# Window attention with a depthwise convolution: x loaded ahead of the convolution, LN by rows of seven tokens, its transposes in the convolution's PSUM banks

## The chip, the cores and the metric

The kernel runs on one core of one Trainium2 chip. A core has TensorE (PE, the matrix engine; PEld is its weight load), VectorE (DVE), ScalarE (ACT), GpSimd (POOL) and SyncE (SP), which here only issues DMAs. SBUF holds tiles of 128 partitions; PSUM holds the results of matmuls, in banks of 512 float32 per partition. The metric is the device time of one execution in microseconds (us), lower is better.

## The reference

The input is an image x of 511 x 511 pixels with 192 channels, in bfloat16. It gets a depthwise 3 x 3 convolution added, and then attention runs inside windows of 7 x 7 pixels, with four heads of 48 channels. The weights are `dw_pe` (3, 3, 192), `w_qkv` (192, 576) and `w_o` (192, 192).

```
xp = pad(x, 1 pixel on each side of H and W)
pe = sum over i, j in 0..2 of xp[:, i:i+H, j:j+W, :] * dw_pe[i, j]
x0 = x + pe
h  = (x0 - mean(x0)) / sqrt(var(x0) + 1e-5)        # over the 192 channels
h  = h cut into windows of 7 x 7                    # 73 x 73 = 5329 windows, 49 tokens each
q, k, v = split(h @ w_qkv)                          # 4 heads of 48
attn = softmax(einsum('wnhd,wmhd->whnm', q, k) * 48 ** -0.5)
out  = einsum('whnm,wmhd->wnhd', attn, v) @ w_o
return x0 + out, windows put back in place
```

## The kernel before

**Blocks.** The 5329 windows are cut into 42 blocks of up to 128 windows (the last has 81). A block's tile `X` is [128 windows, 49 tokens, 192 channels]; there are three of them, `X[b % 3]`. `XP` holds the 9 x 9 pixel patches of a block's windows, with the 81 pixels on the partitions, and `T` holds the convolution as 81 x 49 matrices, one for each channel. So the convolution of a block is 192 matmuls (L308), one a channel; ten of them fill a one-bank PSUM tile `psc` (a ring of two), and DVE casts that tile into `X` (L313).

**LN.** The LN of a block then runs in 7 rows of 7 tokens. For each, DVE adds x to the convolution (L320) from a small buffer `xs` (two of them, one DMA a row, L288), and takes statistics of two tokens at a time (L324, 25 a block). GpSimd turns the variances of sixteen tokens at once into reciprocal roots, with one multiply-add (L330) and one power of -0.5 (L331), and multiplies `X` by them (L339, eight tokens an instruction). The result goes to `X[(b + 1) % 3]`, whose content has been stored by then. The mean isn't subtracted: the weights are made so that it drops out. PE transposes the normalised tokens, eight at a time and in two halves of 96 channels (L353), into one PSUM tile `ps` of two banks (a ring of three, which all of attention uses), and both halves are copied into `HO[b % 2]` (L363), the first by DVE, the second by ACT. Six such steps of 16 transposes and one of two make the 98 of a block.

**Attention.** A block is worked in 16 slots of 8 windows. In a slot PE does, in this order: q (L375), the transposes of an output (E, L458) of two slots ago, k (L375), the output projection of the block before (L470, 13 a block, spread over slots 2 to 10), LN transposes for the next block, attention times v (D, L434) of the slot before, scores (B, L413), and the value projection (V, L391). Each of them takes the next `ps` of the ring. ACT copies q and k (L383) and v (L399) out of PSUM and takes the exponential (`pt`, L421). DVE takes the reciprocal of the sums (L443) and scales the outputs (`o`, L444). The transposed outputs are copied into `HO` (L459) by DVE in slots 0 to 7 and by ACT from slot 8 on (L616: `late = f0 >= 0.44`). A projection is copied by ACT to `pO` (L481; the last of a block has one token, L483), and added to `X` on GpSimd (L485).

**What sets the order.** The instructions are issued by hand in program order; each engine works its own in that order and waits on semaphores. While a block is attended to, the next one is prepared: `fill` puts its convolution matmuls between those of q, k and V, up to 0.44 of the slots; `hook(share)` is called at several places of a slot and issues the LN items (statistics, x loads, GpSimd's work), the stores of the block before (L293, four of them), and the 18 patch loads of the block after the next (L234), on SP's queue, as far as the slot's share says. A transposition is issued when its rows are at least 0.9 slots old.

Of the kernel before, what the change touches and what calls it, by code (L numbers as in the profile page):

```python
# [61 lines left out]
class _Kernel:  # L62
    def __init__(self, ctx, tc, x, dw_pe, w_qkv, w_o, out, eps, logit_lim):
# [24 lines left out]
        with tc.tile_pool(name="setup", bufs=1) as setup:  # L88
# [88 lines left out]
            for t in self.X:  # L177
                nc.gpsimd.memset(t[:], 0.0)
        for t in self.load_xp(0):
            t()  # L180
# [54 lines left out]


    def fast(self, ctx):
# [5 lines left out]
        bnst = pool.tile([128, 25, 6], F32, name="bnst")  # L243
        rstd = pool.tile([128, 50], F32, name="rstd")
        tmp1 = pool.tile([128, 50], F32, name="tmp1")
        expo = pool.tile([128, 50], F32, name="expo")
# [10 lines left out]
        for t in [k_] + xs.t:  # L257
            nc.vector.memset(t[:], 0.0)
# [18 lines left out]
        dram, load_xp = self.dram, self.load_xp  # L277

        def strips(b, r0, r1):

            for a0, b0, da, db, n, p0 in blocks[b]:
                yield slice(p0, p0 + n), (WS * a0 + r0, WS * b0, [[WS * C * (W * da + db), n], [W * C, r1 - r0], [1, WS * C]])

        CHUNKS = [(0, 2), (2, 4), (4, 6), (6, 7)]

        def load_x(b, r, t):
            for p, at in strips(b, r, r + 1):
                nc.sync.dma_start(out=t[p].rearrange("p (r q) c -> p r (q c)", q=WS), in_=dram(x, *at))  # L288
# [27 lines left out]


        def ln_add(b, r, t):
            xv = self.X[b % 3][:, r * WS : (r + 1) * WS, :]
            nc.vector.tensor_tensor(out=xv, in0=xv, in1=t[:], op=ALU.add)  # L320

        def ln_stat(b, i):
            s = min(2 * i, S - 2)
            nc.vector.bn_stats(out=bnst[:, i, :], in_=self.X[b % 3][:, s : s + 2, :].rearrange("p s c -> p c s"))  # L324

        def ln_rstd(i0, i1):
            v = bnst[:, i0:i1, :].rearrange("p a (e f) -> p a e f", f=3)[:, :, :, 2]
            rd, t = (z[:, 2 * i0 : 2 * i1] for z in (rstd, tmp1))
            e = nc.gpsimd
            e.tensor_scalar(out=t.rearrange("p (a e) -> p a e", e=2), in0=v, scalar1=1.0 / C, scalar2=self.eps, op0=ALU.mult, op1=ALU.add)  # L330
            e.tensor_tensor(out=rd, in0=t, in1=expo[:, 2 * i0 : 2 * i1], op=ALU.pow)  # L331

        def hbuf(b):
            return self.X[(b + 1) % 3]

        def ln_norm(b, s0, s1, eng=nc.gpsimd):
            assert b < 2 or stored.get(b - 2, 0) * 2 * WS >= s1 or stored.get(b - 2, 0) == len(CHUNKS)
            i, n = (49 if s0 == S - 1 else s0), s1 - s0
            eng.tensor_tensor(  # L339
                out=hbuf(b)[:, s0:s1, :],  # L340
                in0=self.X[b % 3][:, s0:s1, :],
                in1=rstd[:, i : i + n].unsqueeze(2).to_broadcast([128, n, C]),
                op=ALU.mult,
            )

        def ln_tr(b, s0, n):
            h = hbuf(b)
            ps = PS.next()
            pb = ps[:].bitcast(BF)
            N = min(8, S - s0)  # L350
            for kt in range(2):
                for i in range(N):
                    mm(  # L353
                        pb[0:KT, kt * 1024 + i * 128 : kt * 1024 + (i + 1) * 128],
                        lhsT=h[:, s0 + i, kt * KT : (kt + 1) * KT],
                        rhs=ident[:],
                        start=True,
                        stop=True,
                        is_transpose=True,
                    )  # L360
            for kt in range(2):
                eng = nc.vector.tensor_copy if kt == 0 else nc.scalar.copy
                eng(  # L363
                    out=HO[b % 2][0:KT, kt, :, s0 : s0 + N],
                    in_=pb[0:KT, kt * 1024 : kt * 1024 + N * 128].rearrange("p (s w) -> p w s", w=128),
                )
# [122 lines left out]

        def stat_items(b):  # L490

            tiles = {}
            items = []
            done = 0
            for r in range(WS):
                items.append((1, lambda r=r: ln_add(b, r, tiles[r])))
                last = 25 if r == WS - 1 else (r + 1) * WS // 2
                for i in range(done, last):
                    items.append((0, lambda i=i: ln_stat(b, i)))
                    if i % 8 == 7 or i == 24:  # L500
                        items.append((0, lambda i0=i // 8 * 8, i1=i + 1: ln_rstd(i0, i1)))
                        for s0 in range(i // 8 * 16, min(S, 2 * i + 2), 8):
                            items.append((2, lambda s0=s0: ln_norm(b, s0, min(S, s0 + 8), nc.vector if b == 0 and s0 % 16 else nc.gpsimd)))
                done = last
            return items, tiles

# [5 lines left out]
        class Next:  # L512


            def __init__(n_, b):
                n_.b, n_.conv, n_.si, n_.loaded, n_.tr = b, Conv(b), 0, 0, 0
                n_.items, n_.tiles = stat_items(b)
                n_.ready, n_.due, n_.added = [], [], 0

            def load(n_):  # L520
                if n_.loaded < WS:
                    n_.tiles[n_.loaded] = xs.next()
                    load_x(n_.b, n_.loaded, n_.tiles[n_.loaded])
                    n_.loaded += 1

            def stats(n_, goal):
                while n_.si < goal:
                    kind, it = n_.items[n_.si]
                    if kind == 1 and n_.loaded == n_.added:
                        n_.load()  # L530
                    it()
                    n_.si += 1
                    if kind == 1:
                        n_.added += 1
                    if kind == 2:
                        n_.ready.append(now[0])

            def transpose(n_, goal, age):

                if n_.tr < min(goal, len(n_.ready)) and n_.ready[n_.tr] + age <= now[0]:  # L540
                    ln_tr(n_.b, 8 * n_.tr, n_.tr)
                    n_.tr += 1
                    return True
                return False

        n = Next(0)
        n.load()
        n.load()
        while n.conv.c < C:
            conv_mm(n.conv)  # L550
        if NB > 1:
            for t in load_xp(1):
                t()
        n.stats(len(n.items))
        while n.tr < 7:
            n.transpose(7, -9.0)
        sq = []

        for g in range(NG + LE + 1):
# [6 lines left out]
            if ck == 0:  # L566
                n = Next(b + 1) if b + 1 < NB else None
                xp, xpn = (list(load_xp(b + 2)), 0) if b + 2 < NB else ([], 0)
                pdone = sdone = 0
# [11 lines left out]
            conv_goal = part(0.0, 0.44, C)  # L581
# [10 lines left out]
            s_goal = part(0.46, 0.82, len(n.items)) if n else 0  # L592

            def hook(share):

                nonlocal xpn, sdone
                at = f0 + (f - f0) * share
                if n and conv.c == C:
                    n.stats(int(s_start + (s_goal - s_start) * share))
                    if n.loaded < min(WS, n.added + 2):  # L600
                        n.load()
# [10 lines left out]
            if n and f0 >= 0.3 and n.loaded == 0:  # L612
                n.load()
                n.load()

            late = f0 >= 0.44  # L616
# [3 lines left out]
            if 0 <= g - LE < NG:  # L620
                stage_E(*groups[g - LE], nc.scalar.copy if late else nc.vector.tensor_copy)
# [10 lines left out]
            if n and g < NG:  # L632
                n.transpose(part(0.56, 0.96, 7), 0.9)
            if 0 <= g - LD < NG:
                stage_D()
            if g < NG:
# [3 lines left out]
                if n:  # L640
# [3 lines left out]
                    if f == 1.0:  # L644
                        while n.tr < 7:
                            n.transpose(7, -9.0)
                hook(1.0)
            if f == 1.0:
                while xpn < len(xp):
                    xp[xpn]()  # L650
                    xpn += 1
            if g >= NG:
                hook(1.0)
# [5 lines left out]
    def slow(self, ctx):  # L659
# [25 lines left out]
        nc.vector.memset(XP[:], 0.0)  # L685
# [215 lines left out]
```

## Time and profile before

| | |
|---|---|
| median of 3 runs (lowest to highest) | 4792.46 us (4783.4 to 4797.41) |
| the profiled execution's own time | 4794.51 us |
| its span (first to last instruction) | 4792.8 us |
| mean granted clock of PE, of full speed | 0.863 |
| PE busy | 3893.8 us, 81% |
| PEld busy (beside PE) | 3356.2 us, 70% |
| ACT busy | 3029.9 us, 63% |
| DVE busy | 2722.9 us, 57% |
| POOL busy | 2087.7 us, 44% |

The shares are means over stretches with different limits: a block begins with the convolution as filler for PE and goes on with the LN of the next block. The chain of work that ended last has PE on 56% of the span, ACT on 13%, DVE on 11% and POOL on 8%. Busy time of PE depends on its clock: the same matmuls take longer at the lower level, so a busy share can fall when the clock rises.

### The profile page before, as it was taken

The page shows a single profiled execution, that of the slowest core. Times are in us where ns is not written, and L with a number is a line of the kernel's source. Part 1 is how long each engine was busy: PE and PEld are TensorE (multiplying, and loading weights), DVE is VectorE, ACT ScalarE, POOL GpSimd, SP SyncE. Part 2 cuts the span into 40 slices and gives each one's busy share as a digit, 9 for nine tenths or more (in the row PEclk, how much of TensorE's full clock was granted, in tenths as well). Part 3 has the DMA queues.
Part 4 walks back from the last instruction along what each step waited for, and adds up shares of the span by engine and source line. Part 5 has one row for each costly group of instructions (what it writes and reads, how often), then busy time and mean ns, then how long its engine had stood idle before and what let it go on. Part 6 is the DMA issues. An engine that isn't in the chain of part 4 may idle for free.

```text
span 4792.8 us, 167033 instructions
## 1 busy us (share of the span) xinstructions
PE 3893.8 (81%) x75049; PEld 3356.2 (70%) x75049; DVE 2722.9 (57%) x4200; ACT 3029.9 (63%) x3842; POOL 2087.7 (44%) x1179
## 2 busy tenths in 40 slices
PE   2788888888888888888888888888888888878777
PEld 2677777777777777777777777777777777767665
DVE  5655555565555555555556555555555655555543
ACT  0566666666666666666666666666666666666555
POOL 5244444444444444444444444444444444444333
PEclk9899898888888899899888888889888888888888
DMA  3133333333333333333333333333333333333211
GB/s 93 50 76 76 76 87 81 90 86 89 86 83 76 76 76 76 76 87 82 86 82 87 92 87 76 76 76 76 76 83 80 89 85 77 87 86 78 67 45 35
DMA packets 529704, 376.98 MB, mean 79 GB/s; under 512 B 454181, under 2 KB 454373, under 8 KB 528979
## 3 DMA queue, kind: packets, MB, share of 16 engines
q1 hardware_dynamic: 528513, 365.92, 31.1%
q8 instruction: 589, 9.65, 0.8%
q14 instruction: 136, 1.11, 0.1%
q10 hardware_dynamic: 466, 0.30, 0.0%
HBM read 265.31 MB, written 100.27 MB: 76 GB/s over the span
## 4 chain that ended last, share of the span: by engine, by line
PE 56%; ACT 13%; DVE 11%; POOL 8%; issue 4%; SPq 4%; DMA 3%; ACTq 0%; DVEq 0%; POOLq 0%
PE ps L375 20%; PE ps L391 11%; PE psc L308 9%; PE ps L458 7%; ACT pO L481 6%; DVE HO L363 5%; POOL X L339 5%; ACT HO L363 5%; PE ps L353 4%; PE ps L470 4%; SPq L234 3%; DVE bnst L324 3%; DMA XP<-in_x_dram 3%; DVE X L320 2%; POOL X L485 2%
## 5 line engine op out<-in xcount | busy, mean ns | idle before, releaser
L485 POOL TENSOR_TENSOR X<-X,pO 128x768 bf16<-128x768 bf16 (+1 forms) x539 | 859.5, 1610 | 2322.9 <-ACT pO L481 2321.2
L375 PE MATMUL ps<-HO,Wqk 96*128 96x392 bf16 x5336 | 1632.4, 397 | 113.7 <-DVE o L444 76.2
L308 PEld LDWEIGHTS <-XP 81*128 81x128 bf16 x8064 | 1101.5, 177 | 164.9 <-issue 105.7
L391 PE MATMUL ps<-Wv,HO 96*128 96x192 bf16 x5336 | 718.0, 267 | 485.9 <-ACT HO L363 395.5
L308 PE MATMUL psc<-T,XP 81*128 81x49 bf16 x8064 | 1080.2, 221 | 37.4 <-DMA XP<-in_x_dram 28.2
L375 PEld LDWEIGHTS <-Wqk 96*128 96x128 bf16 x5336 | 656.0, 127 | 321.3 <-issue 211.2
L391 PEld LDWEIGHTS <-HO 96*128 96x128 bf16 x5336 | 556.4, 109 | 450.2 <-issue 419.0
L383 ACT CAST k<-ps 128x784 bf16<-128x784 f32 x667 | 542.8, 814 | 408.5 <-PE ps L375 370.2
L363 DVE COPY HO<-ps 96x1024 bf16<-96x1024 bf16 (+1 forms) x294 | 336.9, 1147 | 784.9 <-ACT k L383 402.5
L383 ACT CAST q<-ps 128x784 bf16<-128x784 f32 x667 | 542.0, 813 | 370.7 <-PE ps L375 329.1
L339 POOL TENSOR_TENSOR X<-X,rstd 128x1536 bf16<-128x1536 bf16 (+1 forms) x291 | 729.8, 2525 | 19.4 <-DMA out_dram<-X 6.2
L399 ACT CAST v<-ps 128x768 bf16<-128x768 f32 x667 | 535.2, 802 | 294.8 <-PE ps L391 262.4
L313 DVE CAST X<-psc 128x490 bf16<-128x490 f32 x840 | 542.4, 646 | 300.9 <-PE psc L308 294.2
L444 DVE TENSOR_TENSOR o<-ps,rs 128x768 bf16<-128x768 f32 x667 | 638.6, 957 | 23.1
L421 ACT ACTIVATE pt<-ps 128x784 bf16<-128x784 f32 x667 | 549.6, 824 | 63.2 <-PE ps L413 60.8
L458 PEld LDWEIGHTS <-o 128*96 128x96 bf16 x5336 | 496.9, 157 | 84.3 <-issue 34.7
L363 ACT COPY HO<-ps 96x1024 bf16<-96x1024 bf16 (+1 forms) x294 | 284.2, 967 | 413.6 <-DVE HO L363 411.3
L324 DVE BATCH_NORM_STATS2 bnst<-X 128x6 f32<-128x384 bf16 x1050 | 528.0, 549 | 10.1
L458 PE MATMUL ps<-ident,o 128*96 128x128 bf16 x5336 | 527.4, 256 | 1.4 <-DVE o L444 1.4
L443 DVE RECIPROCAL rs<-ps 128x16 f32<-128x16 f32 x667 | 167.8, 252 | 537.7 <-PE ps L434 394.0
L470 PE MATMUL ps<-Wo,HO 96*128 96x192 bf16 x4116 | 461.4, 263 | 1.0 <-DVE HO L459 0.7
L470 PEld LDWEIGHTS <-HO 96*128 96x128 bf16 x4116 | 441.5, 183 | 25.8 <-issue 14.6
(58 smaller groups left out, 3498.3 us busy)
## 6 DMA issues: line engine op xcount, KB each, us to landing
XP<-in_x_dram SPq DMA_DIRECT2D x568, 216.0 KB
xs<-in_x_dram SPq DMA_DIRECT2D x574, 168.0 KB
out_dram<-X SPq DMA_DIRECT2D x246, 336.0 KB
XP<-in_x_dram SPq DMA_DIRECT2D x151, 212.6 KB
out_dram<-X SPq DMA_DIRECT2D x82, 168.0 KB
XP<-in_x_dram SPq DMA_DIRECT2D x16, 192.0 KB
XP<-in_x_dram SPq DMA_DIRECT2D x64, 30.4 KB
xs<-in_x_dram SPq DMA_DIRECT2D x63, 23.6 KB
```

Source lines behind the costliest of these rows:

```text
L308: mm(cv.ps[:, (c % 10) * S : (c % 10 + 1) * S], lhsT=XP[0:KP, :, c], rhs=T[0:KP, c, :], start=True, stop=True)
L324: nc.vector.bn_stats(out=bnst[:, i, :], in_=self.X[b % 3][:, s : s + 2, :].rearrange("p s c -> p c s"))
L339: eng.tensor_tensor(out=hbuf(b)[:, s0:s1, :], in0=self.X[b % 3][:, s0:s1, :], in1=rstd[:, i : i + n].unsqueeze(2).to_broadcast([128, n, C] ...
L363: eng(out=HO[b % 2][0:KT, kt, :, s0 : s0 + N], in_=pb[0:KT, kt * 1024 : kt * 1024 + N * 128].rearrange("p (s w) -> p w s", w=128),)
L375: mm(ps[:, ab * 512 : ab * 512 + TOK], lhsT=self.Wqk[kt][0:KT, which * 2 + ab, :], rhs=HO[b % 2][0:KT, kt, ck * CH : (ck + 1) * CH, 0:S], ...
L383: nc.scalar.copy(out=dst[:, :, 0:TOK], in_=two_bank(ps, TOK))
L391: mm(ps[:, col : col + C], lhsT=HO[b % 2][0:KT, kt, w : w + 2, :].rearrange("p w s -> p (w s)"), rhs=self.Wv[kt][0:KT, :], start=(kt == 0) ...
L421: nc.scalar.activation(out=pt[:, 0 : 16 * S].rearrange("p (b n) -> p b n", b=2), in_=two_bank(ps, 8 * S), func=ACTF.Exp, scale=SCALE)
L444: nc.vector.tensor_tensor(out=o_[:].rearrange("p b q (h d) -> p b (q h) d", d=DH), in0=ov[:, :, :, 0:DH], in1=r_[:].rearrange("p (b g) -> ...
L458: mm(ev, lhsT=o_[:, sl, Q, kt * KT : (kt + 1) * KT], rhs=ident[:], start=True, stop=True, is_transpose=True)
L470: mm(ps[:, col : col + C], lhsT=HO[b % 2][0:KT, kt, :, s0 + i], rhs=self.Wo[kt][0:KT, :], start=(kt == 0), stop=(kt == 1))
L485: nc.gpsimd.tensor_tensor(out=xv, in0=xv, in1=o[:, 0:n, :], op=ALU.add)
```

## The change

x is now loaded whole into `X[b % 3]` before the convolution is drained (four DMAs a block, `load_x`), and the drain adds the PSUM tile to it in place of the cast; the buffers `xs` and the separate additions are gone. LN goes by rows of seven tokens: each has its own variance, root and multiply on GpSimd, and the normalised row goes to a ring `h` of two tiles of seven tokens. No more than two rows are ahead of their transposes (`len(n_.ready) - n_.tr < 2`). A row's 14 transposes go to two one-bank tiles of the convolution's ring, one for each half, copied by DVE and ACT as before. Statistics write three values a token. The transposed outputs are copied by DVE in all slots. The x loads of a block are issued behind its 18 patch loads, once the block whose buffer they write is stored; patch loads end at 0.82 of the slots. At the start x of block 0 is loaded with its patches, and `X` is not cleared where a block has all 128 windows.

```
+    def load_x(self, b):
+        nc = self.nc
+        for r0, r1 in ((0, 4), (4, WS)):
+            for p, at in self.strips(b, r0, r1):
+                dst = self.X[b % 3][p, r0 * WS : r1 * WS, :].rearrange("p (r q) c -> p r (q c)", q=WS)
+                yield lambda dst=dst, src=self.dram(self.x, *at): nc.sync.dma_start(out=dst, in_=src)
...
+        hr = _Rot([pool.tile([128, WS, C], BF, name=f"h{i}") for i in range(2)])
-        xs = _Rot([pool.tile([128, WS, C], BF, name=f"xs{i}") for i in range(2)])
...
-                nc.vector.tensor_copy(
-                    out=self.X[cv.b % 3][:, :, c0 : c0 + n], in_=cv.ps[:, 0 : n * S].rearrange("p (c s) -> p s c", s=S)
-                )
-        def ln_add(b, r, t):
-            xv = self.X[b % 3][:, r * WS : (r + 1) * WS, :]
-            nc.vector.tensor_tensor(out=xv, in0=xv, in1=t[:], op=ALU.add)
+                xv = self.X[cv.b % 3][:, :, c0 : c0 + n]
+                nc.vector.tensor_tensor(out=xv, in0=cv.ps[:, 0 : n * S].rearrange("p (c s) -> p s c", s=S), in1=xv, op=ALU.add)
...
+        def ln_norm(b, r, eng):
+            t = slice(r * WS, (r + 1) * WS)
             e = nc.gpsimd
+            e.tensor_scalar(out=tmp1[:, t], in0=bnst[:, t, 2], scalar1=1.0 / C, scalar2=self.eps, op0=ALU.mult, op1=ALU.add)
+            e.tensor_tensor(out=rstd[:, t], in0=tmp1[:, t], in1=expo[:, t], op=ALU.pow)
+            h = hr.next()
             eng.tensor_tensor(
+                out=h[:], in0=self.X[b % 3][:, t, :], in1=rstd[:, t].unsqueeze(2).to_broadcast([128, WS, C]), op=ALU.mult
             )
+        def ln_tr(b, r, h):
+            pb = []
             for kt in range(2):
-                for i in range(N):
+                pb.append(PCB.next()[0:KT, :].bitcast(BF))
+                for i in range(WS):
                     mm(
-                        pb[0:KT, kt * 1024 + i * 128 : kt * 1024 + (i + 1) * 128],
-                        lhsT=h[:, s0 + i, kt * KT : (kt + 1) * KT],
+                        pb[kt][:, i * 128 : (i + 1) * 128],
+                        lhsT=h[:, i, kt * KT : (kt + 1) * KT],
...
             def stats(n_, goal):
+                while n_.si < goal and len(n_.ready) - n_.tr < 2:
+                    n_.items[n_.si]()
                     n_.si += 1
...
-                    goal = part(0.44, 0.92, len(xp), at)
+                    goal = part(0.45, 0.82, len(xp), at)
                     while xpn < goal:
                         xp[xpn]()
                         xpn += 1
+                    if b < 1 or stored.get(b - 1, 0) == len(CHUNKS):
+                        goal = part(0.80, 0.90, len(xl), at)
+                        while xln < goal:
+                            xl[xln]()
+                            xln += 1
...
-                stage_E(*groups[g - LE], nc.scalar.copy if late else nc.vector.tensor_copy)
+                stage_E(*groups[g - LE], nc.vector.tensor_copy)
...
-                n.transpose(part(0.56, 0.96, 7), 0.9)
+                n.transpose(part(0.57, 0.95, WS), 0.9)
```

On ACT, one slot of the second half of a block. A row is the line, the operation, the tile written and the one read, with their buffer numbers, and the shape; `ps0` to `ps2` are the ring of attention. Before:

```order
L459 COPY HO0_247<-ps1_65 96x2x8x49
L383 CAST k_257<-ps2_66 128x2x392
L363 COPY HO1_248<-ps0_64 96x128x8
L421 ACTIVATE pt_259<-ps2_66 128x784
L399 CAST v_258<-ps0_64 128x16x48
L383 CAST q_256<-ps1_65 128x784
```

Now, in such a slot (lines 377, 357, 415 and 393 are 383, 363, 421 and 399 of before):

```order
L377 CAST k_258<-ps1_65 128x2x392
L357 COPY HO0_250<-psc1_68 96x128x7
L415 ACTIVATE pt_260<-ps0_64 128x784
L393 CAST v_259<-ps1_65 128x16x48
L377 CAST q_257<-ps2_66 128x784
```

Before, v is read from the tile that the transposes were read from (`ps0`); now v is read from the tile that k was read from (`ps1`), and the transposes stand in `psc1`. The output copy (L459) is no longer on ACT.

On POOL, the LN of a block among the adds of the projections of the block before (`X` by number: one is the block under LN, the other the block before it). Before:

```order
L330 TENSOR_SCALAR tmp_253<-bnst 128x16
L331 TENSOR_TENSOR rstd<-tmp_253,expo 128x16
L339 TENSOR_TENSOR X_78<-X_77,rstd 128x1536 x2
L485 TENSOR_TENSOR X_78<-X_78,pO_262 128x768
L485 TENSOR_TENSOR X_78<-X_78,pO_261 128x768
L485 TENSOR_TENSOR X_78<-X_78,pO_262 128x192
L330 TENSOR_SCALAR tmp_253<-bnst 128x16
```

Now (lines 334, 335, 337 and 479 are 330, 331, 339 and 485 of before):

```order
L334 TENSOR_SCALAR tmp_254<-bnst 128x7
L335 TENSOR_TENSOR rstd<-tmp_254,expo 128x7
L337 TENSOR_TENSOR h_248<-X_76,rstd 128x1344
L479 TENSOR_TENSOR X_77<-X_77,pO_263 128x768
L334 TENSOR_SCALAR tmp_254<-bnst 128x7
L335 TENSOR_TENSOR rstd<-tmp_254,expo 128x7
L337 TENSOR_TENSOR h_249<-X_76,rstd 128x1344
L479 TENSOR_TENSOR X_77<-X_77,pO_262 128x768
L479 TENSOR_TENSOR X_77<-X_77,pO_263 128x768
L334 TENSOR_SCALAR tmp_254<-bnst 128x7
```

One row of LN stands between the first adds where there were two multiplies of eight tokens, and the multiply writes `h` and not an `X`.

## Rows read from the trace of the kernel before

**Rows 1.** Windows: start:end and length; each engine's busy us (x), PEclk, DMA, GB/s
```profile
132.10:4703.60 4571.50, 3789.50 (x73488) 3266.01 (x73488) 2617.51 (x4055) 2963.44 (x3760) 1982.64 (x1135) 0.86 0.32 79
2117.60:2165.45 47.85, 45.30 (x966) 42.96 (x966) 27.44 (x45) 32.45 (x42) 14.73 (x9) 0.98 0.18 46
2165.45:2227.00 61.55, 45.66 (x836) 35.77 (x834) 36.32 (x55) 40.10 (x52) 34.16 (x19) 0.82 0.45 111
...
4455.40:4592.80 137.40, 95.30 (x1799) 82.25 (x1799) 63.27 (x99) 73.67 (x93) 47.79 (x28) 0.81 0.23 55
...
2202.72:2208.68 5.96, 4.36 (x107) 3.61 (x106) 2.34 (x3) 4.68 (x7) 5.51 (x5) 1.00 0.64 162
```

**Rows 2.** Waits: who waited for whom, us in total, times, longest us
```profile
ACT HO L363 <- DVE HO L363: 411.3, 212, 96.6
...
PE ps L391 <- ACT HO L363: 395.5, 246, 6.2
...
PE ps L391 <- ACT pO L481: 90.2, 318, 1.1
```

**Rows 3.** Timeline 2195 to 2209: start us, us, engine, line, operation [idle before <-releaser]
```profile
2195.26 1.51 PE L375 MATMUL ps<-HO,Wqk 96*128 96x392 bf16 x4
...
2202.06 0.82 PE L391 MATMUL ps<-Wv,HO 96*128 96x192 bf16 x8 [1.79 <-ACT HO L363]
...
2202.72 0.84 PE L375 MATMUL ps<-HO,Wqk 96*128 96x392 bf16 x4
...
2205.70 1.22 DVE L363 COPY HO<-ps 96x1024 bf16<-96x1024 bf16 x1 [3.10 <-PE ps L353]
...
2206.95 1.01 ACT L363 COPY HO<-ps 96x1024 bf16<-96x1024 bf16 x1 [1.04 <-DVE HO L363]
...
2208.01 0.87 PE L391 MATMUL ps<-Wv,HO 96*128 96x192 bf16 x8 [1.60 <-ACT HO L363]
...
2208.68 0.53 PE L375 MATMUL ps<-HO,Wqk 96*128 96x392 bf16 x1
```

**Rows 4.** Lines by form: operation and count | busy us, mean ns | idle before, releasers
```profile
L485 POOL TENSOR_TENSOR X<-X,pO 128x768 bf16<-128x768 bf16 x498 | 837.4, 1695 | 2321.3 <-ACT pO L481 2321.2
...
L313 DVE CAST X<-psc 128x490 bf16<-128x490 f32 x798 | 531.6, 666 | 294.4 <-PE psc L308 288.6 <-issue 2.5
L324 DVE BATCH_NORM_STATS2 bnst<-X 128x6 f32<-128x384 bf16 x1050 | 528.0, 549 | 10.1
...
L331 POOL TENSOR_TENSOR rstd<-tmp,expo 128x16 f32<-128x16 f32 x126 | 387.5, 3075 | 10.5
...
L320 DVE TENSOR_TENSOR X<-X,xs 128x1344 bf16<-128x1344 bf16 x294 | 348.1, 1184 | 52.1 <-DMA xs<-in_x_dram 50.5
...
L459 ACT COPY HO<-ps 96x784 bf16<-96x784 bf16 x334 | 277.4, 831 | 0.0
...
L459 DVE COPY HO<-ps 96x784 bf16<-96x784 bf16 x333 | 192.3, 577 | 322.3 <-PE ps L458 314.6 <-ACT q L383 7.7
...
L331 POOL TENSOR_TENSOR rstd<-tmp,expo 128x2 f32<-128x2 f32 x42 | 29.2, 696 | 3.5
...
L485 POOL TENSOR_TENSOR X<-X,pO 128x192 bf16<-128x192 bf16 x41 | 23.5, 574 | 1.6 <-ACT pO L483 1.6
...
L475 DVE TENSOR_TENSOR X<-ps,X 128x384 bf16<-128x384 f32 x12 | 6.1, 553 | 4.9 <-PE ps L470 4.9
```

**Rows 5.** Timeline of POOL, 2063 to 2098
```profile
2066.73 6.07 POOL L339 TENSOR_TENSOR X<-X,rstd 128x1536 bf16<-128x1536 bf16 x2
...
2091.97 5.46 POOL L339 TENSOR_TENSOR X<-X,rstd 128x1536 bf16<-128x1536 bf16 x2
```

**Rows 6.** Timeline of SP's queue, 60 to 83
```profile
60.38 22.04 SPq L234 DMA_DIRECT2D XP<-in_x_dram  x18
```

**Rows 7.** The page's list of DMA issues: transfer, queue, count, KB each
```profile
XP<-in_x_dram SPq DMA_DIRECT2D x568, 216.0 KB
```

**Rows 8.** Timeline of DVE, 80 to 100
```profile
89.62 0.86 DVE L320 TENSOR_TENSOR X<-X,xs 128x1344 bf16<-128x1344 bf16 x1 [23.42 <-DMA xs<-in_x_dram]
```

More of the change, by code (lines that the diff above doesn't have):

```diff
@@ L333, in hbuf @@
[L333 to L338, printed above, removed]
+            nc.vector.bn_stats(
+                out=bnst[:, s : s + 2, :].rearrange("p a f -> p (a f)"),
+                in_=self.X[b % 3][:, s : s + 2, :].rearrange("p s c -> p c s"),
+            )
+        def ln_norm(b, r, eng):
+            t = slice(r * WS, (r + 1) * WS)
+            e = nc.gpsimd
+            e.tensor_scalar(out=tmp1[:, t], in0=bnst[:, t, 2], scalar1=1.0 / C, scalar2=self.eps, op0=ALU.mult, op1=ALU.add)
+            e.tensor_tensor(out=rstd[:, t], in0=tmp1[:, t], in1=expo[:, t], op=ALU.pow)
+            h = hr.next()
@@ L488, in fast @@
         stored = {}
[L490 to L505, printed above, removed]
         groups = [(b, ck) for b in range(NB) for ck in range((count(b) + CH - 1) // CH)]
@@ L515, in __init__, with norm, finish @@
             def __init__(n_, b):
[L516 to L524, printed above, removed]
-            def stats(n_, goal):
[L527 to L531, printed above, removed]
+                n_.b, n_.conv, n_.si, n_.tr = b, Conv(b), 0, 0
+                n_.ready, n_.items = [], []
+                done = 0
+                for r in range(WS):
+                    last = ((r + 1) * WS + 1) // 2
+                    n_.items += [lambda i=i: ln_stat(b, i) for i in range(done, last)]
+                    n_.items.append(lambda r=r: n_.norm(r))
+                    done = last
+            def norm(n_, r):
+                eng = nc.vector if n_.b == 0 and r % 2 else nc.gpsimd
+                n_.ready.append((now[0], ln_norm(n_.b, r, eng)))
+            def stats(n_, goal):
+                while n_.si < goal and len(n_.ready) - n_.tr < 2:
+                    n_.items[n_.si]()
                     n_.si += 1
[L533 to L536, printed above, removed]
             def transpose(n_, goal, age):
-                if n_.tr < min(goal, len(n_.ready)) and n_.ready[n_.tr] + age <= now[0]:
-                    ln_tr(n_.b, 8 * n_.tr, n_.tr)
+                if n_.tr < min(goal, len(n_.ready)) and n_.ready[n_.tr][0] + age <= now[0]:
+                    ln_tr(n_.b, n_.tr, n_.ready[n_.tr][1])
                     n_.tr += 1
-                    return True
-                return False
+            def finish(n_):
+                while n_.tr < WS:
+                    n_.stats(len(n_.items))
+                    n_.transpose(WS, -9.0)
         n = Next(0)
-        n.load()
-        n.load()
         while n.conv.c < C:
@@ L551, in fast @@
         if NB > 1:
-            for t in load_xp(1):
+            for t in list(load_xp(1)) + list(load_x(1)):
                 t()
-        n.stats(len(n.items))
-        while n.tr < 7:
-            n.transpose(7, -9.0)
+        n.finish()
         sq = []
@@ L591, in fast @@
             s_start = n.si if n else 0
-            s_goal = part(0.46, 0.82, len(n.items)) if n else 0
+            s_goal = part(0.46, 0.83, len(n.items)) if n else 0
             def hook(share):
-                nonlocal xpn, sdone
+                nonlocal xpn, xln
                 at = f0 + (f - f0) * share
@@ L644, in fast @@
                     if f == 1.0:
-                        while n.tr < 7:
-                            n.transpose(7, -9.0)
-                hook(1.0)
+                        n.finish()
+            hook(1.0)
             if f == 1.0:
[L649 to L653, printed above, removed]
+                for t in xp[xpn:]:
+                    t()
+                if sq and b < NB:
+                    while sq:
+                        _, bb, k = sq.pop(0)
+                        store(bb, k)
+                        stored[bb] = k + 1
+                for t in xl[xln:]:
+                    t()
+                xpn, xln = len(xp), len(xl)
         while sq:
```

61 lines of the change are left out of this document (21 added, 40 removed).

## The prediction

> **What bounds the kernel now.** I read the stretches first, then the waits of TensorE (PE), then one slot in order of time, then durations. A slot is one group of eight windows; 16 slots make a block, and 41 blocks carry work for a following block.
>
> The stretches [rows 1] show that the blocks are what matters: 4571.50 us of the 4792.8, a mean of 111.5 for each of the 41. The block of 2117.60 to 2227.00 takes 109.4 and splits in two. In slots 0 to 7, with the convolution as filler, PE is busy 45.30 of 47.85 us at a granted clock of 0.98. In slots 8 to 15, where the next block's LN is done, it is busy 45.66 of 61.55 at 0.82, for a smaller load (836 matmul records against 966). So the first half is bound by PE; in the second PE waits, and its clock falls.
>
> What it waits for [rows 2]: the value projection for a copy on ScalarE (ACT), 395.5 us in 246 waits, and that copy for the same transposes' copy on VectorE (DVE), 411.3. The slot from 2202.72 shows it [rows 3]: the DVE copy out of the transposes runs 2205.70 to 2206.92, the ACT copy 2206.95 to 2207.96, and only then the value projection starts (2208.01, after 1.60 of waiting), because it needs the PSUM buffer of the transposes, three allocations back in a ring of three. The next query matmul then takes 0.53 us alone, where the four of 2202.72 took 0.84 together: the lower clock level, 1.2 of 2.4 GHz, after a wait. But the wait of 1.79 at 2202.06 left the clock up: such a wait costs the clock sometimes.
>
> **The change part by part.** The sum is made against the profiled run (4794.51 us, span 4792.8), 0.04% above the median.
>
> *Transposes in the convolution banks.* PE still issues 98 a block and ACT and DVE still drain 98, now in seven pairs of 14. The value projection then needs the buffer of a projection or of k, not of the transposes, and the ACT copy no longer stands behind the DVE copy, since each has its own tile. The 395.5 us go, 9.6 a block. A slot from query matmul to query matmul was 5.96 [rows 1, 3]; without 1.60 it is 4.36, as much as PE is busy in it [rows 1]. ACT follows: it is busy 4.68 there; less the slot's output copy, 0.83 [rows 4], and an eighth of the transpose copy of 1.01, 3.72 are left.
>
> *Output copies on DVE in slots 8 to 15.* ACT loses 0.831 a slot, DVE gains 0.577 [rows 4]. DVE was busy 2.34 in that slot with the transpose copy of 1.22, the reciprocal and o [rows 1, 3]; an eighth of the copy goes, 0.15, this copy and three or four statistics of 0.549 come [rows 4]: 4.4 to 5.0. The o that the next query matmul waits for stands last in that queue, so DVE paces slots 10 to 14 at about 4.7 to 5.0, and PE waits some 0.6 there.
>
> *The x adds.* 294 additions of 1.184 us leave DVE [rows 4], 348 us in all or 8.5 a block, all from slots 8 to 12. In exchange the 19 drains of 490 elements in a block get a second operand: 0.666 as a cast. The nearest row of PSUM plus SBUF is 384 elements in 0.553 [rows 4], which scaled to 490 is 0.71: the upper guess, and 0.67 the lower. For the farthest end I take twice the cast, 1.33, as if both operands were read one after the other: 2.4 drains a slot would add 1.6 us, 13 a stage, to a DVE busy 27.44 of 47.85 [rows 1], which still fits. Below nothing it can't be, since the drain does more. I take 0.70, at no cost while that room lasts.
>
> *LN by rows on POOL.* A reciprocal root of 16 took 3.075 and of 2 0.696 [rows 4]; on that line one of 7 is 1.55. The multiply of two took 6.07 in one place and 5.46 in another [rows 5]; 7/8 of a half is 2.66 or 2.39. I take 2.39, which is the commoner, and 2.66 is the other end (+1.9 a block). The Trainium skill (GPSIMD Engine Reference, 1. Specifications) says that POOL shares its SBUF interfaces with VectorE and contends with instructions that have two SBUF inputs there. The x adds were such instructions, and by that rule all rows would now cost 2.39. With 0.2 for the variance and 0.07 for the steps between, a row is 4.3, seven are 30.
>
> **The LN stage, walked.** Time 0 is the first query matmul of slot 8, all at full clock. Three statistics are done by then, the fourth stands behind the output copy, so row 0 starts on POOL at 2.4. POOL's order is row 0, one add of 1.65, row 1, two adds, row 2, the small add of 0.57, rows 3 to 6 (adds by [rows 4]): rows end at 6.7, 12.7, 20.3, 25.2, 29.5, 33.9 and 39.1 (the last waits for its statistics, which stand behind o of slot 13). PE: slot 8 4.4; slot 9 6.3 with two projections; slot 10 5.0, its ACT queue held about 0.7 by the small output copy, which waits for the first of the two adds (until 14.3) with the transpose copy, exp and v behind it; slot 11 reaches its transposes at 18.1 and waits for row 2 until 20.3; slot 12 starts at 23.2, 13 at 28.1, 14 at 32.8, 15 at 37.4; its transposes come at 39.2 and it ends at 41.8. So POOL is late next, once hard (2.2 us) and then just behind.
>
> To 41.8 I add 1.5 for one fall of the clock after the 2.2: the slot from 2195.26 to 2202.72, whose four matmuls took 1.51 where the next slot's took 0.84, was 7.46 long against 5.96 [rows 3]. And 2.0 for eight small waits of 0.25 that the walk doesn't have, the size of PE's short waits for ACT (90.2 in 318) [rows 2]. That is 45.3 for 61.55. The convolution stage was 47.85 here; with fewer blocks that begin it at the low clock I take 47.4, a guess. Block: 92.7.
>
> *Loads.* Four x loads replace 14. They stand behind all eighteen patch loads on SP, whose issue is 22.04 for eighteen [rows 6], 1.22 each. SP sends eight by the end of the convolution, three behind the store that waits for the adds (16), seven behind the store of the small add (21): to 31. The x bytes, 128 partitions by seven rows of 1344, 2.4 MB, at the patch loads' rate (216.0 KB in 1.22 us [rows 6, 7]) are 14 us: 45, where the next convolution's first drain is due at 45.3 + 2.5. Just in time; hidden by the last three slots, and its price when they don't hide it is the fourth rival.
>
> *Edges.* The start loses DVE's 23.42 wait for x [rows 8]; row-wise work is paced by POOL there too, so I take 22. The block from 4455.40 stays at its 137.4 [rows 1], since it loads patches in small pieces to its end: 45 over a block of 92.7. I allow 12 for the block before it, which has small pieces too, a guess: together 57. Three memsets on POOL go at the start, beside other work: nothing.
>
> **Sum:** 41 x 92.7 + 57 = 3858 against 4571.5, minus 713.5; minus 22; 4794.5 becomes 4059, say 4060.
>
> **Rivals.**
> - *POOL dearer.* Root a fifth above the line, 2.66 for the multiply, adds half a microsecond dearer: 0.3 and 0.27 on seven rows and 0.5 on three adds, 5.5 a block, 4285. For: the multiply of 6.07 [rows 5]; against: the x adds are gone from DVE.
> - *The clock keeps falling.* PE waits 0.6 to 0.8 twice a slot. If that drops it to the lower level, five more slots pay 1.5 each: 7.5 a block, 4365. Against: the wait of 1.79 that left it up [rows 3]. The Trainium skill (TensorE: Matmul & The Clock Gate, A second HAM failure mode: psum-queue depth-cycling) says that frequent short idling between groups of matmuls that cycle through PSUM makes the clock swing between its levels; this is that rival, and the trace shows both outcomes.
> - *Nothing else waits.* 41.8 and 46.9 a block, no fall and no small waits: 88.7, 3895.
> - *x comes late.* The change adds a wait of DVE's drains for the x loads; behind one stand the output copy, reciprocal and o, and so PE. Each microsecond past 47.8 costs 41. The gain is 18.8 a block by the mean, so from 19 late the kernel is slower: the 2.4 MB would need 36 us, 67 GB/s. At 25 us late: 4060 + 41 x 25 = 5085. Against: the LN stage moves 111 GB/s on average now [rows 1], patch loads with it.
> - *No change:* the value projection still waits as long for its new buffer's drain, and the kernel stays at 4794. Against: that copy (k) ends before the scores start.
>
> **Chances.** Forecast 0.50 (3960 to 4170), POOL dearer 0.18, clock 0.14, nothing else waits 0.11, x late 0.05 of which 0.03 slower, no change 0.02. The runs of before lie within 0.2% of their median, so 0.3% is what can be told: faster 0.95, same 0.02, slower 0.03. The range 3900 to 4380 leaves out the last two, and some of the third and second.
>
> **What would show it.** Right: no wait of the value projection for the transpose copies; slots 12 to 15 under 5.2; transposes waiting for POOL about once a block for 2 us; drains at 0.67 to 0.71; granted clock over 0.93. Wrong: drains that wait for x loads; the lower clock level in slots 12 to 15; POOL idle in slots 9 to 14, which would mean that DVE or ACT sets the pace.

## The result, and the profile after

The changed kernel takes 4285.77 us in the median of 4 runs (4256.8 to 4287.61) against 4794.93 for the kernel before: a ratio of 0.8927, 95% interval 0.8885 to 0.8968. The forecast was 4060, in a range of 3900 to 4380. The direction and the range held; the gain is 509 us where 735 were forecast.

The profiled run took 4284.34 us. The stretches of the same kind as [rows 1] (start:end and length; busy us and instructions of PE, PEld, DVE, ACT, POOL; granted clock, DMA share, GB/s): all blocks, the two halves of one of them, and 13 us in its last slots.

```profile
104.10:4200.20 4096.10, 3537.68 (x73488) 3093.01 (x73488) 2451.07 (x4096) 2716.10 (x3431) 1981.97 (x1381) 0.91 0.38 88
2036.27:2083.96 47.69, 44.52 (x966) 42.65 (x966) 27.21 (x46) 32.34 (x42) 14.74 (x9) 1.00 0.15 36
2083.96:2135.52 51.56, 41.86 (x837) 33.30 (x835) 32.56 (x56) 34.12 (x45) 34.08 (x25) 0.87 0.64 146
2115.00:2128.00 13.00, 8.32 (x195) 6.61 (x194) 7.57 (x13) 7.63 (x10) 8.24 (x6) 0.87 1.03 202
```

The convolution half is as long as before (47.69 against 47.85). The LN half fell from 61.55 to 51.56, not to 45.3. In its last slots the DMA engines are busy all the time (1.03; packets are counted where they start, so a share can pass 1).

The waits, as [rows 2]: who waited for whom, us in total, times, longest.

```profile
PE psc L347 <- POOL h L337: 122.3, 84, 7.1
...
PE ps L385 <- ACT pO L475: 95.4, 321, 1.1
...
PE ps L369 <- DVE o L438: 91.0, 207, 0.8
...
PE psc L314 <- DMA XP<-in_x_dram: 53.9, 5, 13.5
DVE X L320 <- DMA X<-in_x_dram: 53.3, 9, 8.4
PE ps L407 <- issue: 49.8, 15, 4.5
PE psc L314 <- DMA X<-in_x_dram: 48.7, 3, 37.7
```

The wait of the value projection for the transposes' copy, 395.5 us before, isn't among them any more; what PE waits for in that stage is POOL (2.35 us once a block, below) and o (0.8 at most). New are waits with the releaser "issue": PE waits for nothing that the profile shows, in the midst of a group of matmuls.

Where the slots' lengths are told from here on, they are the times between the starts of ACT's copies of q. Medians of slots 8 to 15:

```
           8     9     10    11    12    13    14    15
before    7.17  6.40  9.78  8.26  6.82  6.63  7.13  8.57
walked    4.4   6.3   5.0   7.5   4.9   4.7   4.6   4.4
after     4.51  6.32  5.48  8.02  5.38  4.70  4.87  8.32
```

The walk holds to within 0.5 us up to slot 14 (it leaves out the 1.5 and 2.0 that the prediction adds behind it). Slot 11's wait for POOL, forecast as 2.2 us once a block, is there 40 times with 2.35 (timeline; the idle time stands in brackets):

```profile
1817.99 1.49 POOL L335 TENSOR_TENSOR rstd<-tmp,expo 128x7 f32<-128x7 f32 x1
...
1819.56 2.44 POOL L337 TENSOR_TENSOR h<-X,rstd 128x1344 bf16<-128x1344 bf16 x1
...
1822.05 0.98 PE L347 MATMUL psc<-ident,h 128*96 128x128 bf16 x14 [2.35 <-POOL h L337]
```

POOL's third row ended 20.6 us after the first query matmul of slot 8 (20.3 in the walk). The durations by form, as [rows 4]:

```profile
L479 POOL TENSOR_TENSOR X<-X,pO 128x768 bf16<-128x768 bf16 x498 | 814.2, 1649 | 1853.9 <-ACT pO L475 1853.9
L337 POOL TENSOR_TENSOR h<-X,rstd 128x1344 bf16<-128x1344 bf16 x291 | 707.7, 2432 | 22.8
...
L320 DVE TENSOR_TENSOR X<-psc,X 128x490 bf16<-128x490 f32 x798 | 530.6, 665 | 313.5 <-PE psc L314 249.6 <-DMA X<-in_x_dram 53.3 <-issue 0.3
...
L335 POOL TENSOR_TENSOR rstd<-tmp,expo 128x7 f32<-128x7 f32 x294 | 436.7, 1485 | 24.5
```

All are at or near the cheap end of their bounds: the drain with its second operand costs what the cast did (665 ns against 666), the root 1.49 (1.55 forecast), the multiply 2.43 (2.39). The 291 multiplies on GpSimd all took 2.427 to 2.443; before, those of eight tokens took from 2.75 to 4.32. Every row has one price, as the prediction expected once the x additions are gone.

What the walk doesn't have stands in slots 14 and 15. In the block above (timelines of SP and of PE):

```profile
2113.54 3.18 SPq L250 DMA_DIRECT2D X<-in_x_dram  x4
```
```profile
2121.70 0.26 PE L385 MATMUL ps<-Wv,HO 96*128 96x192 bf16 x1
2126.09 1.28 PE L385 MATMUL ps<-Wv,HO 96*128 96x192 bf16 x7 [4.14 <-issue]
2127.17 1.51 PE L369 MATMUL ps<-HO,Wqk 96*128 96x392 bf16 x4
```

One of eight matmuls of a value projection runs, then PE stands still for 4.14 us, and after it the clock is at the lower level (1.51 for four query matmuls). The trace's packets show what came late:

```
packets of the instruction queue (16384 bytes each): 2111.98 for 1.25, 2123.30 for 1.30, 2127.91 for 1.22
packets of 2688 bytes (x) started per 2 us from 2113: 0 60 117 160 151 158 162 87 1
```

PE goes on 1.49 us after the end of the instruction packet at 2124.60, which ran among the packets of the x loads. Slots 14 and 15 have 30 such gaps of over half a microsecond, in 29 of the first 34 blocks, up to 4.52 us, 85.6 in all; every one of them ends 1.25 to 1.73 us after an instruction packet does. The Trainium skill (Runtime: NRT & Kernel Launch, Instruction fetch mechanics) says that an engine fetches the next 16 KiB of its instructions over a DMA queue of its own while it works on the current ones, and that this is mostly hidden. The size agrees with these packets; hidden it is not here.

The trace ties the gaps to the pieces more closely. Number all records of PE and PEld from the first one: each of these gaps ends at the record whose number is 256 times the packets landed so far, plus 193. So PE's instructions come in pieces of 256 records, a packet each, and it is at the start of a piece that PE stands still. From the record that starts one piece to the start of the packet for the next it is 0.72 us in the median of the first 34 blocks (476 packets). It is over 4 us for 34 packets (4.03 to 7.18), one in each of these blocks, among its x packets. In the kernel before it is never over 3.4 us there.

### The profile page after: what moved, and what is told of

Same layout as the page of the kernel before. It is cut to its first block, busy times and chain, and to the rows that moved or that the text cites. A ratio compares the mean times of both kernels' runs of the same rounds, so it can differ in the third digit from the quotient of the medians.

```text
span 4282.5 us, 166362 instructions
## 1 busy us (share of the span) xinstructions
PE 3637.9 (85%) x75049; PEld 3180.5 (74%) x75049; DVE 2548.2 (60%) x4238; ACT 2779.9 (65%) x3508; POOL 2061.2 (48%) x1428
## 3 DMA queue, kind: packets, MB, share of 16 engines
q14 instruction: 131, 1.07, 0.1%
## 4 chain that ended last, share of the span: by engine, by line
PE 51%; POOL 15%; DVE 10%; ACT 9%; SPq 6%; issue 5%; DMA 3%; ACTq 0%; POOLq 0%; DVEq 0%
PE ps L369 17%; PE psc L314 10%; PE ps L385 8%; POOL h L337 6%; ACT pO L475 6%; PE ps L452 6%; SPq L236 5%; POOL X L479 4%; PE ps L464 4%; POOL rstd L335 4%; DVE o L438 3%; PE psc L347 3%; DMA X<-in_x_dram 3%; DVE bnst L325 2%; ACT k L377 2%
## 5 line engine op out<-in xcount | busy, mean ns | idle before, releaser
L369 PE MATMUL ps<-HO,Wqk 96*128 96x392 bf16 x5336 | 1454.5, 357 | 100.1 <-DVE o L438 91.0
L453 DVE COPY HO<-ps 96x784 bf16<-96x784 bf16 x667 | 381.9, 573 | 614.9 <-PE ps L452 551.2
L320 DVE TENSOR_TENSOR X<-psc,X 128x490 bf16<-128x490 f32 x840 | 541.4, 645 | 321.6 <-PE psc L314 257.6
L337 POOL TENSOR_TENSOR h<-X,rstd 128x1344 bf16<-128x1344 bf16 x291 | 707.7, 2432 | 22.8
L385 PEld LDWEIGHTS <-HO 96*128 96x128 bf16 x5336 | 520.7, 107 | 122.5 <-issue 94.0
L357 DVE COPY HO<-psc 96x896 bf16<-96x896 bf16 x294 | 339.0, 1153 | 323.8 <-PE psc L347 322.1
L452 PEld LDWEIGHTS <-o 128*96 128x96 bf16 x5336 | 422.1, 137 | 53.8 <-issue 8.6
L452 PE MATMUL ps<-ident,o 128*96 128x128 bf16 x5336 | 456.2, 234 | 3.9 <-issue 2.5
L357 ACT COPY HO<-psc 96x896 bf16<-96x896 bf16 x294 | 324.1, 1102 | 194.1 <-PE psc L347 152.1
L335 POOL TENSOR_TENSOR rstd<-tmp,expo 128x7 f32<-128x7 f32 x294 | 436.7, 1485 | 24.5
```

The lines of the kernel that those rows point to most:

```text
L335: e.tensor_tensor(out=rstd[:, t], in0=tmp1[:, t], in1=expo[:, t], op=ALU.pow)
L337: eng.tensor_tensor(out=h[:], in0=self.X[b % 3][:, t, :], in1=rstd[:, t].unsqueeze(2).to_broadcast([128, WS, C]), op=ALU.mult)
L357: eng(out=HO[b % 2][0:KT, kt, :, r * WS : (r + 1) * WS], in_=pb[kt][:, 0 : WS * 128].rearrange("p (s w) -> p w s", w=128),)
L369: mm(ps[:, ab * 512 : ab * 512 + TOK], lhsT=self.Wqk[kt][0:KT, which * 2 + ab, :], rhs=HO[b % 2][0:KT, kt, ck * CH : (ck + 1) * CH, 0:S], ...
L385: mm(ps[:, col : col + C], lhsT=HO[b % 2][0:KT, kt, w : w + 2, :].rearrange("p w s -> p (w s)"), rhs=self.Wv[kt][0:KT, :], start=(kt == 0) ...
L452: mm(ev, lhsT=o_[:, sl, Q, kt * KT : (kt + 1) * KT], rhs=ident[:], start=True, stop=True, is_transpose=True)
```

## The experiments

Ratios are against the kernel before, with 95% intervals. A plain block is one of the first 34.

**x_none: no x loads after the first three blocks.**
```
-                xl, xln = (list(load_x(b + 2)), 0) if b + 2 < NB else ([], 0)
+                xl, xln = (list(load_x(b + 2)), 0) if b < 1 else ([], 0)
```


> The changed kernel without the x loads of blocks 3 to 41 (their buffers keep what they held, so x is left out of the sum there; every other instruction stays). Theory: the burst of four x loads at the end of a block fills the DMA engines, PE's next instructions come late behind it, and PE stands still for 2 to 4.5 us in slot 14 or 15 of 28 blocks, after which its clock falls. Without the loads these gaps are gone, slots 14 and 15 take 4.9 and 4.7 in the median instead of 4.9 and 8.3, and blocks 34 to 40, where SP issues 37 patch loads before the x loads, gain some us each: 4080 to 4160 us. Rival, PE uses up its instructions faster than they are fetched, whatever else is loaded: the gaps stay, 4230 to 4290 us.

4071.37 us, 0.8475 (0.8421 to 0.8530), nine below the range of the theory. One gap is left of 30, in block 0, which still loads x, and there stands the only packet that is over 4 us late (6.72); slot 15 takes 5.39 in the median, a plain block 92.1 where the sum said 92.7. Two halves of a block (windows as above):

```profile
1670.04:1716.69 46.65, 44.04 (x966) 42.37 (x966) 27.22 (x46) 32.37 (x41) 14.74 (x9) 1.00 0.13 32
1716.69:1762.15 45.46, 39.38 (x837) 31.81 (x835) 32.67 (x56) 33.92 (x44) 34.10 (x25) 0.92 0.45 113
```

45.46 is the 45.3 of the forecast, though not slot by slot: slot 11 takes 8.88 for the 7.5 walked, since the clock falls behind the wait for POOL (granted 0.67 in the median of this slot, 0.79 in the changed kernel), and slot 15 takes 5.39 for 4.4. The time that was missing hangs on the x loads; PE doesn't outrun its instructions by itself.

**x_split: half of x earlier.**
```
-                    if b < 1 or stored.get(b - 1, 0) == len(CHUNKS):
-                        goal = part(0.80, 0.90, len(xl), at)
+                    if b < 1 or stored.get(b - 1, 0) >= 2:
+                        goal = part(0.54, 0.66, len(xl) // 2, at)
+                        if b < 1 or stored.get(b - 1, 0) == len(CHUNKS):
+                            goal = max(goal, part(0.80, 0.90, len(xl), at))
```


> The changed kernel with the first two of a block's four x loads (rows 0 to 3, 1344 KB) issued in slots 8 to 10, once the stores of those rows are issued, and only the last two (1008 KB) behind the patch loads. Theory of the burst: less than half of it stands at the end, the gaps shrink or go in most blocks, 4150 to 4230 us. Rival 1, any fully loaded stretch delays the instructions: the gaps move to slots 9 to 12 and the time stays within 20 us of 4286. Rival 2, the early x loads push the patch loads back, and the convolution's first matmul waits for them: slower, over 4300 us.

4153.95 us, 0.8646 (0.8590 to 0.8702), as the theory of the burst has it: a plain block takes 93.2 with all its bytes, slot 15 5.40 in the median, and the gaps in slots 14 and 15 are 21.4 us in 14 (all from the profiled run, which took 4177.88). So most of the harm is not in the load, but in that it stands at one place. Rival 1 is seen on a small scale: five gaps, 7.7 us, are new in slots 10 and 11. Rival 2 is seen in the last seven blocks alone, 818 us for 796. Six of them issue more than the usual 18 patch loads (27, three times 36, 34 and 81, beside a few that clear an edge), and SP comes to them later.

**p_dir: two projections added by DVE.**
```
-                proj(b - 1, s0, b == NB and s0 % 8 == 0)
+                proj(b - 1, s0, s0 % 8 == 0 if b == NB else s0 >= 44)
```


> The changed kernel with the last two projections of a block added to X by DVE straight from PSUM (three additions), without the ACT copies and the GpSimd additions. It takes 2.2 us from GpSimd between the first and the third row of LN and puts some 1.5 us on DVE in slot 10. Theory, GpSimd alone holds the transposes of slot 11 (2.35 us, with a fall of the clock behind it): the wait is gone, slot 11 falls from 8.0 to 5 to 6 us, slot 10 grows by up to 1, 4180 to 4240 us. Rival, DVE is as full as GpSimd there and takes all of it: 4275 to 4330 us.

4225.24 us, 0.8805 (0.8743 to 0.8868). Slot 11 falls from 8.02 to 6.00; its wait for POOL shrinks from 2.35 to 0.94 in the median. Slot 12 gains 0.7, since no fall of the clock follows: the granted clock of slots 11 and 12 is 1.00 in every one of blocks 1 to 33, 0.79 and 0.84 on average in the changed kernel. Slot 10 gains 0.6; the small projection's copy on ACT, which waited there 1.05 us for GpSimd's addition, is gone. Slot 9 grows by 0.4. POOL held that place, as the walk had it. But the gaps of PE stay, 85.0 us in all, some now in slot 0 (slots 0 and 1 take 14.6 together, 12.6 in the changed kernel), which ate a part.

**u_ps: the transposes back in attention's ring.**
```
-            pb = []
+            ps = PS.next()
+            pb = []
...
-                pb.append(PCB.next()[0:KT, :].bitcast(BF))
+                pb.append(ps[0:KT, kt * 512 : (kt + 1) * 512].bitcast(BF))
```


> The changed kernel with the 14 transposes of a row put back into one tile of attention's ring of three (each half in its own bank), the rest unchanged. Theory: taking the transposes out of the ring was what removed the wait of the value projection; with them back it waits for the ACT copy again, 1 to 1.8 us in seven slots, 6 to 10 us a block: 4530 to 4690 us. Rival, the lighter ACT (no output copies) and smaller rows were what removed it: 4270 to 4360 us.

4507.40 us, 0.9392 (0.9332 to 0.9452): just under the range of the theory, far from the rival's. The old wait is back:

```profile
PE ps L386 <- ACT HO L358: 446.6, 284, 2.1
```

A plain block takes 103.0, 5.9 over the changed kernel's and 10.9 over x_none's. The wait is worth about what the prediction took (9.6); in the slower stage PE's gaps in slots 14 and 15 are only 10.9 us in 6, so that undoing it seems to cost less against the changed kernel.

**b_tr: the kernel before with this one part.** The same exchange as above, the other way round, for eight tokens a tile.


> The kernel before with one part of the change alone: its LN transposes (still eight tokens at a time) go to two one-bank tiles of the convolution's ring, one for each half. Theory: this alone removes the wait of the value projection for the ACT copy (395.5 us in all, and some falls of the clock with it), and nothing else is late enough to take its place, since ACT with the output copies is busy 4.6 us a slot: 4350 to 4480 us. Rival, the later limits of the old LN (output copies on ACT, x additions on DVE) take half of it: 4550 to 4650 us.

4548.71 us, 0.9496 (0.9435 to 0.9556), a microsecond below the rival's range: the rival was right by its number. The value projection's waits for the copy are gone, and this one has grown (before, then with the banks):

```profile
PE ps L375 <- DVE o L444: 76.2, 46, 1.9
```
```profile
PE ps L375 <- DVE o L444: 285.1, 217, 5.2
```

o stands on DVE behind the x additions: in four fifths of this waiting one of them is among the last six instructions that DVE ran without a pause before o. So the banks alone bring half of the gain (239 us of 509); by these waits it is x on DVE that holds back the rest, which no run of its own shows.

**u_eact: output copies back on ACT.**
```
-                stage_E(*groups[g - LE], nc.vector.tensor_copy)
+                stage_E(*groups[g - LE], nc.scalar.copy if f0 >= 0.44 else nc.vector.tensor_copy)
```


> The changed kernel with the output copies of slots 8 to 15 back on ACT. By the working of the prediction ACT is then busy 4.5 us a slot and DVE 3.9 to 4.4, both about as long as PE's 4.36 to 4.7, so the LN stage keeps its length: 4260 to 4330 us. Rival, the copy stands between those of q and k, the scores wait for k, and each slot of the stage grows by 0.3 to 0.8: 4370 to 4550 us.

4249.52 us, 0.8891 (0.8850 to 0.8932). That is ten below the range of the theory, and the interval overlaps the changed kernel's: this part of the change is worth nothing, as expected.

**u_ps_eact: both undone.** The two edits above together.


> The changed kernel with both undone, the transposes in attention's ring and the output copies of slots 8 to 15 on ACT; what is left of the change is x loaded ahead and LN by rows. Theory: in the ring the value projection waits for the last copy on ACT, and the output copy on ACT delays it by its 0.83: 0.3 to 0.8 a slot more than with the transposes alone undone (4507), 4590 to 4750 us. Rival, the output copies cost nothing on either engine: 4480 to 4530 us.

4517.77 us, 0.9444 (0.9409 to 0.9478): the rival. The copies cost nothing with the transposes in the ring either; the theory that they delay the transposes' copy is wrong. This run is also the other half of b_tr: x loaded ahead and LN by rows without the banks take 270 us off (27 of them at the start), the banks without them 239, and the changed kernel 509. So the two halves add up and neither needs the other; x ahead and LN by rows were not taken apart.

**best: x_split (not in the blocks with more than 18 patch loads) and p_dir.** Both edits above, the first with this in place of its second added line:
```
+                        goal = part(0.54, 0.66, len(xl) // 2 if len(xp) < 20 else 0, at)
```


> The changed kernel with the first two x loads of a block in slots 8 to 10 (not in the blocks with 37 patch loads), and the last two projections of a block added by DVE from PSUM. If the two effects add up, a plain block takes 92 less 2.9 in slots 9 to 12, and the last blocks stay as in the changed kernel: 4010 to 4070 us. Rival, the shorter LN stage brings the rest of the loads closer to its end, and the gaps of PE come back: 4090 to 4160 us.

4071.23 us, 0.8496 (0.8470 to 0.8521), a microsecond over the sum's range. The commonest block takes 89, the mean of the plain ones 91.0. Slots 14 and 15 have one gap of PE left, but the early x loads bring some in other slots (21.7 us in 18 altogether). The last seven blocks take 792.

**col_act: best, and a third of the patch loads in those last blocks issued by ACT.** The loads take the engine as an argument, and:
```
+                        xp[xpn](e=nc.scalar if len(xp) > 20 and xpn % 3 == 2 else nc.sync)
```


> The kernel of the last run of the call before (first x loads in slots 8 to 10, two projections added by DVE, 4071 us), with every third patch load of the blocks that have 37 of them issued by ACT in place of SP. Theory: in the five blocks from the 35th on SP issues these loads one behind the other up to the block's end, and the next convolution waits for the last; with a second queue these blocks fall from some 115 us to 95 to 105: 3980 to 4040 us. Rival, the transfers themselves are the limit, or ACT loses as much time with the issues as SP saves: 4055 to 4100 us.

4027.63 us, 0.8413 (0.8362 to 0.8465). In the changed kernel one of these blocks ends so (SP, then PE):

```profile
3701.53 20.38 SPq L236 DMA_DIRECT2D XP<-in_x_dram  x15
3722.02 4.23 SPq L250 DMA_DIRECT2D X<-in_x_dram  x4
```
```profile
3728.31 0.35 PE L314 MATMUL psc<-T,XP 81*128 81x49 bf16 x2 [13.30 <-DMA XP<-in_x_dram]
```

With two queues SP is done with the same block's patch loads 42.9 us after the first (3468.19 to 3511.12), where it took 51.1 (3670.85 to 3721.91), and the last seven blocks take 743 us for 792. The expectation's five blocks don't come down to its 95 to 105: they take 106.2, 106.0, 106.8, 116.2 and 111.4 (116.9, 114.4, 115.3, 112.9 and 138.1 in best). Twelve of its loads stand on ACT's queue, such as

```profile
3467.42 0.70 ACTq L236 DMA_DIRECT2D XP<-in_x_dram  x1
```

The Trainium skill (DMA: Bandwidth & Descriptors, Issuing engines are not separate DMA queues) says that issuing from several engines saves only the time of issuing, usually small beside the transfer. Here this time is a good part of the limit, since half of these loads are of one window; the DMA engines of the changed kernel were busy 0.48 of that half block. It is not all of it: with two queues PE still waits for such loads, up to 10.9 us at a time.

## Why the prediction came out as it did

Against the profiled runs, the forecast and the trace, part by part:

```
                        forecast          after
start                   110.1             104.1
34 plain blocks         34 x 92.7 = 3152  3300    (97.06 each)
last seven blocks       7 x 92.7 + 57 = 706  796
end                      90.9              84.1
sum                     4059              4284
```

- *The banks*: right. The wait went and the next one was POOL's in slot 11, at 2.35 for 2.2; undone, it costs 10.9 a plain block against the undisturbed 92.1, with 9.6 forecast for the wait itself.
- *Output copies on DVE*: they were costed as a shift that makes DVE pace slots 10 to 14 at 4.7 to 5.0, and slots 13 and 14 are 4.70 and 4.87. But u_eact, with these copies back on ACT, has the same 4.70 and 4.87, so the agreement doesn't show that they set the pace. That the shift itself is worth nothing the prediction didn't say.
- *The x additions*: at no cost in the drains, right. Their removal had no term of its own beyond the wait for o; b_tr suggests, by its waits for o, that without it DVE takes half of the gain back, and u_ps_eact measures 270 us for it together with LN by rows.
- *LN by rows*: right to 0.1 us a row.
- *Loads*: this step failed: "Just in time; hidden by the last three slots, and its price when they don't hide it is the fourth rival". The sum asked only who waits for x. x came in time in the plain blocks, where the drains waited 6.1 us for it in all. But its burst kept PE's instructions away, a load that the forecast had on no list. The forecast missed 4.4 a block, 148 us in the plain blocks; without the loads (x_none) a plain block is 4.9 shorter, nearly all of it in slots 14 to 1: 21.2 for 26.0 us. PE idles 2.0 us less in them, and the other 2.9 are the lower clock behind the gaps.
- *Edges*: mis-sized, 57 for 147 over plain blocks of 92.7 (796 less 649). The forecast gave one block 45 and the others 12; there are six of over 100, since 36 patch loads and more keep SP's queue for 51 us, longer than the shortened stage was to take. Without x loads these seven still take 748, so of the miss of 90 x is 48; the other 42 stay without x, and col_act, which shortens the issue of the patch loads, takes 49 off the same blocks of best.
- *Rivals*: "POOL dearer" named 4285, which is the time by chance; POOL's operations were not dearer. "The clock keeps falling" did not happen in the waits of 0.5 to 0.7 before the query matmuls: after the one of 0.71 at 1825.14 four matmuls take 0.84, and slot 13 has a granted clock of 1.00 in each of blocks 1 to 33. "x comes late" was right about the resource and wrong about who waits.
- *The signs*: the transposes' wait for POOL came once a block at 2.35, and the drains took 0.67. The granted clock is 0.91, where over 0.93 was to show that the forecast is right, and slots 12 (5.38) and 15 (8.32) are over 5.2: the clock falls behind the wait for POOL and behind the late instructions.

Two things that look odd are settled by the traces. Slots 0 and 1 take 12.6 us for 10.8 in x_none; PE is idle 0.84 us in them in both, so the difference is the clock alone (0.80 for 1.00). And five of the first 34 blocks have no gap in slots 14 and 15, though their packet is as late as the others' (4.0 to 6.1 us): in two the gap falls in the next block's slot 0 (1.01 and 0.53 us), in two it is under half a microsecond (0.46 and 0.27), and in one it is 2.41 us before a convolution matmul and listed under x. PE loses the part of the delay that the rest of its current piece doesn't cover.

What stays open: why the instruction packet starts so late behind the x packets. The trace has when a packet starts, but not when it was asked for, nor what it queued behind. And what sets the 4.70 and 4.87 of slots 13 and 14.

## What to carry to other kernels

Before you call a DMA hidden, list everything that shares the DMA engines, the engines' own instructions among it: an engine that issues matmuls fast needs its next piece in time, and a burst of some 13 us in front of it stopped it here where no semaphore shows. Spread a load over the stretch where the DMA engines are idle, instead of putting it in one piece behind the last store. And when a stage gets shorter, recount what has to be issued in it: a queue that had time before can become the bound.

## What the runs showed of the hardware

- PE goes on 1.25 to 1.73 us after its late instruction packet has ended, in all 30 gaps, however long they are (0.8 to 4.52 us), and always at the start of a piece of 256 records. The packet for the next piece starts 0.72 us (median; 0.46 in x_none) after PE has begun the current one: one piece ahead.
- The two copies out of the transposes' banks take 1.29 to 1.30 us each in the median in slots 11 and 14, where they run side by side for 0.9 us (82 pairs), and 1.09 and 0.91 or 1.02 in slots 9 and 10, where they run one after the other. Side by side for 0.7 us (slots 12 and 13) they take 1.07 to 1.12 in the median, so the overlap alone doesn't explain it. One pair after the other, and one side by side:

```profile
1809.81 1.09 DVE L357 COPY HO<-psc 96x896 bf16<-96x896 bf16 x1 [1.91 <-PE psc L347]
1810.99 0.91 ACT L357 COPY HO<-psc 96x896 bf16<-96x896 bf16 x1
...
1822.68 1.30 DVE L357 COPY HO<-psc 96x896 bf16<-96x896 bf16 x1 [3.19 <-PE psc L347]
1823.07 1.29 ACT L357 COPY HO<-psc 96x896 bf16<-96x896 bf16 x1 [2.47 <-PE psc L347]
```

  They read different banks and write different halves of `HO`. GpSimd's root (L335) also runs for over half a microsecond beside 83 of the 84 copies on DVE that took over 1.25 us (here from 1822.75 to 1824.24), and beside 60 of the 210 others; what slows them was not tested.
- A drain that adds PSUM to SBUF took what the cast took, 665 against 666 ns for 490 elements.
